# Reordering the first loads, an early load of x, and a rebuilt tail in an attention and GLU kernel

**Chip, cores, metric.** One core of one Trainium2 chip. The metric is device time in microseconds (us) of one launch. The profiled span is about 1.8 us shorter than the time of the same run (367.0 and 368.85 before).

## The reference, cut to what matters

```python
x  = A_x                                     # 1 x 2048 x 640, bf16
xn = _layernorm(x, axis=-1)
s  = _A_ref(xn, wq, wk, wv, wo, beta)        # 4 segments of 512 rows, 32 heads of 20:
                                             #   causal softmax attention in the segment
                                             #   + linear memory M, z of the segments before, gated by beta; then @ wo
g  = _silu(_B_ref(xn, w_gate, w_up, w_down)) # h = sigmoid(xn @ w_gate) * (xn @ w_up), 640 -> 1536 -> 640
return x + s * g
```

## The kernel before

Everything stands in one hand-made order per engine. A segment's attention is cut into 8 head groups of 3 units, so 24 slots per segment and 96 in all. Each slot issues the scores of one unit, the exponentials (ScalarE), planned items of the next segment, and "dense" items (gate, up and down projections) until the planned TensorE time of the slot is reached. A few functions matter here.

```python
# head: x in four pieces, then whole weights on the SP queue; Wg and Wu on the ACT queue
load_x(0, split=4)
load_w(nc.sync, Wv, A_wv); load_w(nc.sync, Wk, A_wk); load_w(nc.sync, Wq, A_wq)
# ... (cut)
for j in range(4):
    ln_transpose(0, j, xns[j], nc.scalar)
    if j < 2:
        keep_warm(3)                                   # dummy matmuls
        w, src = ((Wg, B_w_gate), (Wu, B_w_up))[j]
        load_w(nc.scalar, w, src)
    if j >= 1:
        for half in range(2):
            do_V(0, j - 1, half, nc.scalar)
# ... V of tile 3, three K groups, three Q groups (cut)
spill(0, 1, nc.sync, nc.sync)
bound(0, 1, None)
k_tok(0)            # transposing DMA
load_x(1)           # x of segment 1
do_gate(0, 0)
do_up(0, 0)
```

```python
def do_up(n, f):    # 5 matmuls into a PSUM tile; hT frees it. Three such tiles serve all dense work
    # ... (cut)
    nc.vector.scalar_tensor_tensor(out=h[:], in0=seg[n]["tg"][:], scalar=1.0, in1=up[:], op0=ALU.add, op1=ALU.mult)

# segment_plan: what slot s of segment n does for segment m = n + 1
for j in range(4):
    at(j, 0, stats, j)          # VectorE: statistics of row tile j of x
    at(4 + j, 0, norm, j)       # VectorE: normalise, then store to DRAM
at(7, 0, ln_dmaT, m)            # transposing DMA of the whole segment
```

```python
total = sum(...)                                 # planned ns of all items, dense ones too
rate = total / (NSEG * NSLOT)                    # planned TensorE ns per slot
# in every slot:
    scores(g, UNITS[ui]); pt = exps(ui, UNITS[ui])
    due += rate
    run(small); fill(due - rate / 2)             # fill: dense items until the planned time done reaches its argument
    if pend is not None: attend(*pend)           # attention of the unit before
    run(big)
    # ... (cut)
    fill(due)
# after the last slot
fill(1e12)
for j in range(4): tail_T(j)                     # transposes of the first 4 of 5 column blocks
for i in range(2): tail_mm(i)
attend(*pend)                                    # the last unit: 2 of 4 row tiles
for i in range(2, 6): tail_mm(i)
tail_end()                                       # add, last column block, last matmuls, then 8 mults and 4 adds;
                                                 # three of the adds on GpSimd, one on VectorE
```

## Time and profile before

| | before |
|---|---|
| time, first 4 runs | 369.57 us median (368.58 to 370.38) |
| profiled run | span 367.0 us |
| first scores start, 5th unit's scores start | 33.09, 49.06 |
| scores of the last (96th) unit start | 349.67 |
| from there to the end of the span | 17.33 |

In the lines of the profile PE is TensorE's matmuls, DVE VectorE, ACT ScalarE, POOL GpSimd, and SPq the DMA queue of SyncE. Sps holds the scores, pt their exponentials, Aps the attention sums, odot the finished attention, gp and up the gate and up products, tg the tanh of gp, hT the product that goes into the down projection (yp), po and oT the transposed attention.

The starts are read from the timeline of the matmuls that write the scores. They cut the span in three: a head up to the fifth unit, by which the hole at 40 us and its slow clock are over; a middle, in which TensorE (PE) is the bound; and a tail.

### The profile page before, as it was taken

How to read it: one execution, taken by the hardware profiler on the slowest of the kernel's cores; microseconds unless marked ns; L12 is line 12 of the kernel's file. 1: busy time of each engine (PE TensorE's matmuls, PEld its weight loads, DVE VectorE, ACT ScalarE, POOL GpSimd, SP SyncE). 2: the span in 40 equal slices, each digit the busy share in tenths (PEclk: the TensorE clock that was granted, in tenths of full speed). 3: DMA queues.
4: the chain of work that ended last, by engine and by line, in shares of the span. 5: the costliest groups of instructions: out<-in, count | busy, mean ns of one | idle time of the engine just before them, and what ended most of it. 6: DMA issues, size and time to landing. Idle time of an engine off the chain costs nothing.

```text
span 367.0 us, 8227 instructions
## 1 busy us (share of the span) xinstructions
PE 340.2 (93%) x3346; PEld 186.2 (51%) x3389; DVE 221.1 (60%) x499; ACT 224.4 (61%) x234; POOL 104.7 (29%) x172
## 2 busy tenths in 40 slices
PE   7999799999999898999999899999989999999992
PEld 2633344655554444555466345555436644555661
DVE  5373566554656984775746986856655573554444
ACT  2424488656776665556677666466867666666540
POOL 7600242222223242222142432222222232322224
PEclk9999899999999999999999999999999999999998
DMA  7976781311483117121393026111402023001001
GB/s 230 384 272 162 173 307 56 73 45 43 103 168 80 56 38 175 41 79 64 102 174 76 36 80 173 36 62 63 133 1 75 2 74 73 18 22 35 2 1 71
DMA packets 48309, 35.40 MB, mean 96 GB/s; under 512 B 25360, under 2 KB 46992, under 8 KB 48272
## 3 DMA queue, kind: packets, MB, share of 16 engines
q1 hardware_dynamic: 46960, 30.95, 30.4%
q10 hardware_dynamic: 1312, 3.93, 2.7%
q8 instruction: 26, 0.43, 0.5%
q14 instruction: 11, 0.09, 0.1%
HBM read 17.05 MB, written 11.80 MB: 79 GB/s over the span
## 4 chain that ended last, share of the span: by engine, by line
PE 65%; ACT 11%; DMA 7%; DVE 7%; issue 3%; SPq 3%; POOL 2%; POOLq 0%; ACTq 0%; DVEq 0%
PE yp L375 13%; PE up L361 11%; PE gp L352 9%; ACT pt L475 8%; PE Aps L491 7%; PE psq L224 6%; PE Sps L467 6%; PE sp L402 4%; PE psv L282 4%; DMA Kd<-ktd 2%; DMA Wv<-in_A_wv_dram 2%; DMA oT<-Od 1%; DMA xt<-in_A_x_dram 1%; POOL pt L477 1%; PE dm L318 1%
## 5 line engine op out<-in xcount | busy, mean ns | idle before, releaser
L475 ACT ACTIVATE pt<-Sps 128x2048 bf16<-128x2048 f32 (+1 forms) x96 | 152.9, 1592 | 50.7 <-PE Sps L467 49.9
L477 POOL TENSOR_SCALAR_AFFINE_SELECT pt<-pt 128x512 bf16<-128x512 bf16 x128 | 83.7, 664 | 247.2 <-ACT pt L475 247.0
L361 PE MATMUL up<-xnT,Wu 128*128 128x512 bf16 x225 | 58.9, 380 | 5.9 <-ACT tg L355 3.0
L352 PE MATMUL gp<-xnT,Wg 128*128 128x512 bf16 x228 | 59.4, 384 | 2.9 <-ACT tg L355 1.8
L375 PE MATMUL yp<-Wd,hT 128*128 128x320 bf16 x384 | 57.5, 299 | 0.0
L491 PEld LDWEIGHTS <-pt 128*128 128x128 bf16 x1280 | 44.3, 96 | 23.3 <-issue 4.9
L364 DVE SCALAR_TENSOR_TENSOR hT<-tg,up 128x512 bf16<-128x512 bf16 x48 | 32.6, 680 | 37.7 <-PE up L361 32.7
L491 PE MATMUL Aps<-V,pt 128*128 128x21 bf16 x1280 | 47.6, 173 | 4.1 <-DVE odot L503 1.9
L375 PEld LDWEIGHTS <-hT 128*128 128x128 bf16 x384 | 35.1, 97 | 14.9 <-issue 2.0
L355 ACT ACTIVATE tg<-gp 128x512 bf16<-128x512 f32 x48 | 28.6, 595 | 22.5 <-PE gp L352 18.9
L379 DVE SCALAR_TENSOR_TENSOR aa<-t,yp 128x320 bf16<-128x320 bf16 x32 | 15.6, 487 | 40.4 <-ACT t L378 40.3
L467 PE MATMUL Sps<-QT,KT 21*128 21x128 bf16 (+3 forms) x512 | 35.1, 303 | 1.1 <-ACT pt L475 0.8
L361 PEld LDWEIGHTS <-Wu 128*128 128x128 bf16 x240 | 21.0, 97 | 27.5 <-issue 8.5
L352 PEld LDWEIGHTS <-Wg 128*128 128x128 bf16 x240 | 20.7, 98 | 24.3 <-issue 5.9
L467 PEld LDWEIGHTS <-KT 21*128 21x128 bf16 x512 | 11.5, 91 | 33.0 <-issue 32.6
L282 PE MATMUL psv<-Wv,xnT 128*128 128x320 bf16 x160 | 26.1, 299 | 0.8 <-DMA Wv<-in_A_wv_dram 0.8
L287 ACT CAST V<-psv 128x320 bf16<-128x320 f32 x32 | 13.7, 428 | 20.4 <-PE psv L282 20.2
L224 PE MATMUL psq<-xnT,Wq 128*128 128x512 bf16 x92 | 23.7, 378 | 1.0 <-DMA Wq<-in_A_wq_dram 0.5
L224 PE MATMUL psq<-xnT,Wk 128*128 128x512 bf16 x92 | 23.6, 378 | 0.5
L378 ACT ACTIVATE t<-yp 128x320 bf16<-128x320 f32 x32 | 14.0, 437 | 16.3 <-PE yp L375 16.2
L229 DVE CAST ktd<-psq 128x512 bf16<-128x512 f32 x20 | 13.8, 688 | 14.9 <-PE psq L224 14.8
L402 PE MATMUL sp<-Wo,oT 128*128 128x320 bf16 x120 | 20.2, 298 | 1.3 <-DMA oT<-Od 1.3
(84 smaller groups left out, 316.7 us busy)
## 6 DMA issues: line engine op xcount, KB each, us to landing
KT<-Kd SPq DMA_DIRECT2D x32, 80.0 KB
QT<-Qd SPq DMA_DIRECT2D x32, 80.0 KB
out_dram<-xt SPq DMA_DIRECT2D x16, 160.0 KB
Wg<-in_B_w_gate_dram ACTq DMA_DIRECT2D x1, 1920.0 KB
Wu<-in_B_w_up_dram ACTq DMA_DIRECT2D x1, 1920.0 KB
xt<-in_A_x_dram SPq DMA_DIRECT2D x3, 640.0 KB
Wd<-in_B_w_down_dram SPq DMA_DIRECT2D x1, 1920.0 KB
Xd<-xn SPq DMA_DIRECT2D x12, 160.0 KB
```

Source lines behind the costliest of these rows:

```text
L224: nc.tensor.matmul(ps[:], lhsT=W[:, k, c * P:(c + 1) * P], rhs=xnT_of[n][:, k, :], start=(k == 0), stop=(k == DC - 1))
L282: nc.tensor.matmul(ps[:], lhsT=xnT_of[n][:, k, j * P:(j + 1) * P], rhs=Wv[:, k, half * HD:(half + 1) * HD], start=(k == 0), stop=(k == DC ...
L352: nc.tensor.matmul(gp[:], lhsT=Wg[:, k, f * P:(f + 1) * P], rhs=xnT_of[n][:, k, :], start=(k == 0), stop=(k == DC - 1))
L355: nc.scalar.activation(tg[:], gp[:], ACT.Tanh, scale=0.5)
L361: nc.tensor.matmul(up[:], lhsT=Wu[:, k, f * P:(f + 1) * P], rhs=xnT_of[n][:, k, :], start=(k == 0), stop=(k == DC - 1))
L364: nc.vector.scalar_tensor_tensor(out=h[:], in0=seg[n]["tg"][:], scalar=1.0, in1=up[:], op0=ALU.add, op1=ALU.mult)
L375: nc.tensor.matmul(yp[:], lhsT=s["hT"][f][:, j * P:(j + 1) * P], rhs=Wd[:, f, hs], start=(f == 0), stop=(f == FC - 1))
L402: nc.tensor.matmul(sp[:], lhsT=s["oT"][:, c, j * P:(j + 1) * P], rhs=Wo[:, c, hs], start=(c == 0), stop=(c == DC - 1))
L467: nc.tensor.matmul(Sps[:, r, c0:c0 + ncol], lhsT=KT[32 * r:32 * r + E1, g, kb * P:(kb + 1) * P], rhs=QT[32 * r:32 * r + E1, g, q0:L], star ...
L475: nc.scalar.activation(pt[:, :, 0:ntot], Sps[:, :, 0:ntot], ACT.Exp, scale=SCALE)
L477: nc.gpsimd.affine_select(out=pt[:, :, c0:c0 + P], in_=pt[:, :, c0:c0 + P], compare_op=ALU.is_ge, fill=0.0, base=0, pattern=[[0, 4], [1, P ...
L491: nc.tensor.matmul(Aps[:, qb, r, :], lhsT=pt[:, r, off:off + P], rhs=V[n % 2][:, kb, 4 * g + r, :], start=(ui == 0 and r == 0 and qb == 0) ...
```

## The change

The intent is to close holes of PE at both ends. The diff, cut to its core:

```diff
 # head
-    load_x(0, split=4)
-    load_w(nc.sync, Wv, A_wv)
+    for half in range(2):
+        load_x(0, ((2 * half, 2 * half + 1), (2 * half + 1, 2 * half + 2)))
+        hs = slice(half * HD, (half + 1) * HD)
+        nc.sync.dma_start(Wv[:, :, hs], A_wv[:, hs].rearrange("(c p) n -> p c n", p=P))
     ...
+    hold = cpool.tile([P, 1], BF, name="hold")
+    nc.gpsimd.tensor_copy(hold[:], xns[3][:, 0:1])    # GpSimd's constants wait for the last xn
     late_constants()
     ...
-            w, src = ((Wg, B_w_gate), (Wu, B_w_up))[j]
+        else:
+            w, src = ((Wg, B_w_gate), (Wu, B_w_up))[j - 2]
     ...                                               # V: half 0 of all row tiles first, then half 1
 # x of segment 1
     bound_dma(0, 0, [nc.sync])
+    load_x(1)
     ...
     k_tok(0)
-    load_x(1)
     ...
-            at(j, 0, stats, j)
-            at(4 + j, 0, norm, j)
-        at(7, 0, ln_dmaT, m)
+            at(j + (n == 0), 0, stats, j)
+            at(6 + j // 2 if n == 0 else 4 + j, 0, norm, j)
+        at(7 + (n == 0), 0, ln_dmaT, m)
 # two down groups kept back; total, and so rate, is computed without them
     plans = [segment_plan(n) for n in range(NSEG)]
+    held = [dense.pop() for _ in range(2)]
     total = ...
 # tail
+                if n == NSEG - 1 and slot == NSLOT - 1:
+                    tail_add(0, 2, C4, D)             # half the rows of the last group are finished early
     ...
-    fill(1e12)
-    for j in range(4):
-        tail_T(j)
     ...
+    for j in range(4):
+        tail_T(j, nc.vector if j % 2 else nc.scalar)
+    dense.extend(reversed(held))
+    fill(1e12)
+    tail_T4(0, 2); tail_mm(4, 0, DC - 1); tail_mm(5, 0, DC - 1)
+    attend(*pend)
     ...                                               # outputs in order of readiness, the last two adds on VectorE
```

So it has four parts: the head, the early x, the tail, and a side effect of the two held groups on `rate`.

More of the change, by code (lines that the diff above doesn't have):

```diff
@@ L98, with load_x @@
     xt_of, xnT_of = {}, {}
-    def load_x(n, split=1):
-        xt = lnp.tile([P, 4, D], BF, name="xt4", bufs=3)
+    def load_x(n, parts=((0, 4),)):
+        if n not in xt_of:
+            xt_of[n] = lnp.tile([P, 4, D], BF, name="xt4", bufs=3)
         src = x2[n * L:(n + 1) * L, :].rearrange("(j p) d -> p j d", p=P)
-        w = 4 // split
-        for i in range(split):
-            nc.sync.dma_start(xt[:, i * w:(i + 1) * w, :], src[:, i * w:(i + 1) * w, :])
-        xt_of[n] = xt
+        for a, b in parts:
+            nc.sync.dma_start(xt_of[n][:, a:b, :], src[:, a:b, :])
     def load_w(eng, dst, src):
@@ L416, in tail_add, with tail_T @@
         nc.vector.tensor_tensor(t, t, s["omem"][:, j0:j1, c0:c1], op=ALU.add)
-    def tail_T(j):
+    def tail_T(j, eng):
+        if j == 0:
+            tail["oT"] = fpool.tile([P, DC, L], BF, name="oT", bufs=1)
         po = ps_d.tile([P, DC - 1, P], BF, name="po", tag="d")
@@ L421, in tail_T @@
             nc.tensor.transpose(po[:, c, :], seg[NSEG - 1]["odot"][:, j, c * P:(c + 1) * P], ident[:])
-        if j == 0:
-            tail["oT"] = ptp.tile([P, 4, DC - 1, P], BF, name="pt")
-        oT = tail["oT"][:, j]
-        if j % 2:
-            nc.vector.tensor_copy(oT, po[:])
-        else:
-            nc.scalar.copy(oT, po[:])
-    def tail_acc(i):
-        return Sps[:, i, 0:HD] if i < 4 else tail["sp", i][:]
-    def tail_mm(i):
-        if i >= 4:
-            tail["sp", i] = ps_d.tile([P, HD], F32, name="sp", tag="d")
-        hs = slice((i % 2) * HD, (i % 2 + 1) * HD)
-        for c in range(DC - 1):
-            nc.tensor.matmul(tail_acc(i), lhsT=tail["oT"][:, i // 2, c, :], rhs=Wo[:, c, hs],
-                             start=(c == 0), stop=False, skip_group_check=True)
@@ L441, in tail_end @@
-    def tail_end():
-        s = seg[NSEG - 1]
-        tail_add(0, 4, C4, D)
-        po = ps_d.tile([P, 4, P], BF, name="po", tag="d")
-        for j in range(4):
-            nc.tensor.transpose(po[:, j, :], s["odot"][:, j, C4:D], ident[:])
-        oT = fpool.tile([P, DC, L], BF, name="oT", bufs=1)[:, 0, :].rearrange("p (j t) -> p j t", t=P)
-        nc.scalar.copy(oT, po[:])
-        for i in range(8):
-            if i >= 6:
-                tail_mm(i)
-            hs = slice((i % 2) * HD, (i % 2 + 1) * HD)
-            nc.tensor.matmul(tail_acc(i), lhsT=oT[:, i // 2, :], rhs=Wo[:, DC - 1, hs],
-                             start=False, stop=True, skip_group_check=True)
-        for i in range(8):
-            j, hs = i // 2, slice((i % 2) * HD, (i % 2 + 1) * HD)
-            aa, xr = s["aa"][j], xt_of[NSEG - 1][:, j, :]
-            nc.vector.tensor_tensor(aa[:, hs], aa[:, hs], tail_acc(i), op=ALU.mult)
-            if i % 2:
-                eng = nc.vector if j == 3 else nc.gpsimd
-                eng.tensor_tensor(xr, aa[:], xr, op=ALU.add)
-                out_store(NSEG - 1, j)
+        dst = tail["oT"][:, 0:DC - 1, j * P:(j + 1) * P]
@@ new lines, in tail_T, with tail_T4, tail_mm @@
+        if eng is nc.scalar:
+            nc.scalar.copy(dst, po[:])
+        else:
+            nc.vector.tensor_copy(dst, po[:])
+    def tail_T4(j0, j1):
+        po = ps_d.tile([P, 2, P], BF, name="po", tag="d")
+        for j in range(j0, j1):
+            nc.tensor.transpose(po[:, j - j0, :], seg[NSEG - 1]["odot"][:, j, C4:D], ident[:])
+        nc.scalar.copy(tail["oT"][:, DC - 1, j0 * P:j1 * P].rearrange("p (j t) -> p j t", t=P), po[:])
+    def tail_mm(i, c0, c1):
+        if i < 4:
+            tail["sp", i] = ps_d.tile([P, HD], F32, name="sp", tag="d")
+        j, hs = i // 2, slice((i % 2) * HD, (i % 2 + 1) * HD)
+        for c in range(c0, c1):
+            nc.tensor.matmul(tail_acc(i), lhsT=tail["oT"][:, c, j * P:(j + 1) * P], rhs=Wo[:, c, hs],
+                             start=(c == 0), stop=(c == DC - 1), skip_group_check=True)
@@ L464, in scores, with tail_out @@
+    def tail_acc(i):
+        return Sps[:, i - 4, 0:HD] if i >= 4 else tail["sp", i][:]
+    def tail_out(i, eng):
+        s = seg[NSEG - 1]
+        j, hs = i // 2, slice((i % 2) * HD, (i % 2 + 1) * HD)
+        aa, xr = s["aa"][j], xt_of[NSEG - 1][:, j, :]
+        nc.vector.tensor_tensor(aa[:, hs], aa[:, hs], tail_acc(i), op=ALU.mult)
+        if i % 2:
+            eng.tensor_tensor(xr, aa[:], xr, op=ALU.add)
+            out_store(NSEG - 1, j)
     def scores(g, unit):
@@ L494, in attend, with finalize @@
                                      skip_group_check=True)
-        if ui == NU - 1:
-            s = seg[n]
-            if g == 0:
-                s["odot"] = opool.tile([P, 4, D], BF, name="odot", bufs=2)
-            rd = opool.tile([P, 4, 4], F32, name="rd", bufs=3)
-            nc.vector.reciprocal(rd[:], Aps[:, :, :, DH])
-            nc.vector.tensor_tensor(rd[:], rd[:], omg[:, 4 * g:4 * g + 4].unsqueeze(1).to_broadcast([P, 4, 4]),
-                                    op=ALU.mult)
-            nc.vector.tensor_tensor(
-                s["odot"][:, :, 4 * g * DH:(4 * g + 4) * DH].rearrange("p q (r e) -> p q r e", e=DH),
-                Aps[:, :, :, 0:DH], rd[:].unsqueeze(3).to_broadcast([P, 4, 4, DH]), op=ALU.mult)
+        if n == NSEG - 1 and g == NG - 1:
+            if ui:
+                finalize(n, g, 2 * ui - 2, 2 * ui)
+        elif ui == NU - 1:
+            finalize(n, g, 0, 4)
+    def finalize(n, g, q0, q1):
+        s, Aps = seg[n], aps_of[0]
+        if g == 0:
+            s["odot"] = opool.tile([P, 4, D], BF, name="odot", bufs=2)
+        nq = q1 - q0
+        rd = opool.tile([P, 4, 4], F32, name="rd", bufs=3)
+        nc.vector.reciprocal(rd[:, 0:nq, :], Aps[:, q0:q1, :, DH])
+        nc.vector.tensor_tensor(rd[:, 0:nq, :], rd[:, 0:nq, :],
+                                omg[:, 4 * g:4 * g + 4].unsqueeze(1).to_broadcast([P, nq, 4]), op=ALU.mult)
+        nc.vector.tensor_tensor(
+            s["odot"][:, q0:q1, 4 * g * DH:(4 * g + 4) * DH].rearrange("p q (r e) -> p q r e", e=DH),
+            Aps[:, q0:q1, :, 0:DH], rd[:, 0:nq, :].unsqueeze(3).to_broadcast([P, nq, 4, DH]), op=ALU.mult)
     wps = ps_d.tile([P, L], F32, name="wps", tag="d")
@@ L531 @@
             keep_warm(3)
-            w, src = ((Wg, B_w_gate), (Wu, B_w_up))[j]
+        else:
+            w, src = ((Wg, B_w_gate), (Wu, B_w_up))[j - 2]
             load_w(nc.scalar, w, src)
         if j >= 1:
-            for half in range(2):
-                do_V(0, j - 1, half, nc.scalar)
-    for half in range(2):
-        do_V(0, 3, half, nc.scalar)
+            do_V(0, j - 1, 0, nc.scalar)
+    do_V(0, 3, 0, nc.scalar)
+    for j in range(4):
+        do_V(0, j, 1, nc.scalar)
     for c in range(3):
@@ L709 @@
             bound_dma(n + 1, 1, [nc.sync])
+    for j in range(4):
+        tail_T(j, nc.vector if j % 2 else nc.scalar)
+    dense.extend(reversed(held))
     fill(1e12)
-    for j in range(4):
-        tail_T(j)
-    for i in range(2):
-        tail_mm(i)
+    tail_T4(0, 2)
+    tail_mm(4, 0, DC - 1)
+    tail_mm(5, 0, DC - 1)
     attend(*pend)
-    for i in range(2, 6):
-        tail_mm(i)
-    tail_end()
+    tail_add(2, 4, C4, D)
+    tail_mm(0, 0, DC)
+    tail_mm(1, 0, DC)
+    tail_mm(6, 0, DC - 1)
+    tail_mm(7, 0, DC - 1)
+    tail_T4(2, 4)
+    tail_out(0, None)
+    tail_out(1, nc.gpsimd)
+    tail_mm(2, 0, DC)
+    for i in range(4, 8):
+        tail_mm(i, DC - 1, DC)
+    tail_mm(3, 0, DC)
+    tail_out(2, None)
+    tail_out(3, nc.gpsimd)
+    for i in range(4, 8):
+        tail_out(i, nc.vector)
 _INS = ['A_x', 'A_wq', 'A_wk', 'A_wv', 'A_wo', 'A_beta', 'B_x', 'B_w_gate', 'B_w_up', 'B_w_down']
```

## The prediction

> **What bounds the kernel now.** I read the page's busy shares first, then its slices, then the waits, and the timeline only where those showed a hole. Shares and slices of the kernel before:
>
> ```profile
> PE 340.2 (93%) x3346; PEld 186.2 (51%) x3389; DVE 221.1 (60%) x499; ACT 224.4 (61%) x234; POOL 104.7 (29%) x172
> ...
> PE   7999799999999898999999899999989999999992
> ...
> PEclk9999899999999999999999999999999999999998
> ```
>
> TensorE is the bound: 340.2 of 367.0 us busy, 26.8 us idle. Each digit is 9.2 us. The weak slices are the first, the fifth (36.7 to 45.9 us, PE at 7 and the only mid-kernel clock below 9) and the last. The windows view says how much is to be had where: from 46 to 345 us PE works 285.24 of 299.00 us, so nothing that the change does to the ends is lost again there unless PE stalls anew; a microsecond saved before 46 us should stay saved. The waits of the first 46 us name the holes (total us, times, longest):
>
> ```profile
> DVE st L177 <- DMA xt<-in_A_x_dram: 8.3, 2, 6.5
> ...
> PE up L361 <- DVE hT L364: 2.1, 1, 2.1
> ...
> PE psv L282 <- DMA Wv<-in_A_wv_dram: 0.8, 1, 0.8
> PE psq L224 <- DMA Wq<-in_A_wq_dram: 0.5, 1, 0.5
> ```
>
> The second is the big one, and the chain of waits in order of time explains it (start, length, what):
>
> ```profile
> 32.89 2.80 SPq L308
> 35.69 0.05 issue
> 35.74 4.66 DMA xt<-in_A_x_dram
> 40.40 0.02 issue
> 40.42 0.90 DVE st L177 x2
> ...
> 41.47 0.65 DVE hT L364
> 42.12 0.04 issue
> 42.16 1.24 PE up L361 x5
> ```
>
> The load of segment 1's x is issued at 35.74, behind the 2.80 us issue of the transposing DMA. VectorE has the statistics of that x ahead of hT in its program, stands until 40.40, and the PSUM tile that `up` needs is not freed until hT has run. PE is still from 40.06 to 42.16. Then its clock drops (windows view; third from the end is PEclk):
>
> ```profile
> 43.00:44.00 1.00, 1.00 (x19) 0.62 (x18) 1.00 (x3) 0.71 (x1) 0.22 (x1) 0.69 0.59 128
> 44.00:45.00 1.00, 0.78 (x3) 0.41 (x3) 0.96 (x4) 0.00 (x0) 0.42 (x1) 0.50 0.44 41
> 45.00:46.00 1.00, 1.00 (x7) 0.16 (x5) 1.00 (x3) 0.01 (x1) 0.00 (x0) 0.50 0.61 150
> 46.00:47.00 1.00, 1.00 (x6) 0.23 (x3) 0.31 (x2) 0.96 (x2) 0.00 (x0) 0.60 0.99 332
> ```
>
> The missing clock adds up to 0.31 + 0.50 + 0.50 + 0.40 = 1.7 us, some 1.6 us of it while PE had work. The tail (chain, last pieces): the last matmul ends at 361.54, but the add on GpSimd sets the end.
>
> ```profile
> 358.57 0.90 DVE aa L458 x2
> 359.46 0.07 issue
> 359.54 2.74 POOL xt L461 x2
> ```
>
> Three such adds (median 1391 ns each) run until 363.88; the last store is issued at 364.3 and the span ends at 367.0, 2.7 us later.
>
> [...] Wq, on the SP queue, lands only at 19.41, when by my sum of the rates some 6.1 MB had moved, though only 3.1 MB stand on its own queue up to it; the rest was Wg, issued on ACT at 6.76. [...] The normalisation of the fourth tile took 1.95 us beside GpSimd's constants, 0.39 to 0.45 otherwise.
>
> **The change part by part.**
>
> *Head, V.* x tiles 0 and 1, half of Wv, x 2 and 3, the other half, then Wk, Wq; Wg and Wu start after the third and fourth transpose copy (about 10 and 11 us instead of 6.76 and 8.11). Half of Wv then ends after 0.74 MB, reached at about 5.0 us in the windows; before, all of it landed at 9.36. PE was ready at 8.72 and waited 0.78. But the new order (V half, transpose, V half, transpose, V, V) puts one V copy (0.43 us) on ScalarE ahead of each xnT copy (0.69), so V of tile 3 must wait. Walking it: V0 8.72 to 9.40, pT2 to 9.68, xnT2 on ACT 10.05 to 10.75, V copy to 11.2, xnT3 to 11.9, V of tile 3 at 11.95 instead of 11.48. The eight V groups (0.68 each) end at about 15.35 instead of 15.64. Gain: 0.3, not 0.8. The held GpSimd constants save VectorE 1.5 us that PE does not wait for.
>
> *Head, Wq.* Before, with Wg and Wu beside it, the SP queue got about 1.2 of the 4.2 MB that moved from 8.5 to 19.4 us, under a third. In the new kernel about 0.7 MB of Wk and Wq are left when Wg starts; at the same share they take 2.4 MB of traffic, at 390 GB/s 6 us: Wq lands by about 17 us and is needed at 18.6. Gain: 0.5. PE is busy 9.95 of 10 us from 20 to 30, so both shifts pass through: 0.8 us. Total bytes are the same, so the first spill of K, issued about 0.3 us earlier, lands as before (24.8): the first scores (33.09, shifted to 32.3) come near the last row of QT, issued at 29.99 and, at the 2.27 us that the next spill took, landed at about 32.3. I take off 0.1.
>
> *Early load of x.* It is issued at about 30.6 instead of 35.74, lands at about 34, and the statistics come one slot (some 3 us) later, behind hT. The 2.1 us stall goes, and with it the slow clock: 2.1 + 1.6 = 3.7. It pushes the second spill, the transposing DMA and the second half of KT and QT about 1 us later; these are first used some 30 us on. The norms squeezed into slots 6 and 7 are still done before the transposing DMA of slot 8. I take off 0.4 for VectorE, which now has hT, statistics and phi together in slot 4 (about 3.5 us in a slot of 3.1).
>
> *Tail.* Two down groups (1.74 us each) move behind the transposes, attention of the last group is finished for half the rows early, and VectorE takes two of four adds. PE's tail work is unchanged. From the last scores (349.67) PE idles 2.1 us of 11.9 before. After, I count one stall of 0.7 us (a PSUM tile after the transposes), so PE ends about 1.4 earlier, at 360.1. But then VectorE alone has, after the last matmul, five multiplications (0.43 each) and two adds (0.53): about 3.4 us with pipeline gaps, to 363.5, where before the end of GpSimd's work was 363.88. With the same 2.7 us for the last store: gain 0.5, at most.
>
> *Pacing.* The two held groups lower the filling rate per slot by 34 ns of planned time; items shift by up to a group. No sign known; spread of about 1 us.
>
> Sum: 0.8 - 0.1 + 3.7 - 0.4 + 0.5 = 4.5 us. 369.57 - 4.5 = 365.1.
>
> **The rivals.** *A: the stall is replaced.* The early x load stands ahead of the second spill on the same queue; if x comes late all the same, or statistics behind hT delay the next hT, PE waits again and may lose its clock again. For it: the DMA share in 30 to 36 us is already uneven. Against: it is 0.08 in 30 to 31 us, and x then has 6 us. This would leave 1 us of the 3.7: about 368. *B: all holes close and the tail too.* If ScalarE copies faster than I walked, V gains 0.8, and if GpSimd's chain really was the tail's bound, its removal gains 1.5 to 2: about 363. For it: GpSimd ends 2.3 us after the last matmul. Against: the new VectorE queue ends 3.4 us after it. *C: the saving before 46 us is eaten later.* ScalarE (61%) and VectorE (60%) would have to bind in the middle. Against: the middle has PE at 95%. This would make about 368.5.
>
> **Range and chances.** My sum has about 2 us of uncertainty: the clock penalty 1, pacing 1, the tail 0.7, the head 0.5. The four runs before spread over 1.8 us. So 362.7 to 367.3. Faster by over 2% needs 362.2, 7.4 us saved, more than all holes that I count in the parts touched: 0.07. Slower needs a new stall of 12 us: 0.01.
>
> **What would show it.** Right: no wait of `up` for hT at 40 us, clock 1.00 from 40 to 47, the x load issued near 30.6, no wait for Wq, V ending near 15.3 with a wait for xnT of about 0.5; in the tail, PE ending some 3.4 us before VectorE's last add. Wrong: a half clock elsewhere (also in the head, where PE is given less to do), a PE wait for scores or for ktok, more idle time between 46 and 345 us than 13.8 us, or VectorE's tail shorter than 3 us.

## More of the kernel before

The lines of the profile on which the argument rests are in the prediction. One view that it only summed up is needed later: the waits of PE in the middle, here from 46 to 345 us of the kernel before (what waited, for what; us in total, times, longest).

```profile
PE up L361 <- ACT tg L355: 3.0, 4, 1.6
PE Aps L491 <- DVE odot L503: 1.9, 3, 0.8
PE gp L352 <- ACT tg L355: 1.8, 2, 1.3
...
PE Sps L467 <- ACT pt L475: 0.8, 2, 0.4
```

Gate and up groups wait for a PSUM tile that ScalarE's tanh has not yet read (tg): 4.8 us in 6 waits.

## The result and the profile after

| | before | after |
|---|---|---|
| time, median (range, fast runs) | 370.08 (368.58 to 371.67, 16 runs) | 362.09 (361.59 to 363.59, 10 runs; an eleventh fast one, 364.00, is not counted) |
| ratio of the fast runs | | 0.979 (0.977 to 0.981) |
| span of the profiled run | 367.0 | 360.0 |
| first scores, 5th unit's scores | 33.09, 49.06 | 31.83, 44.58 |
| last unit's scores | 349.67 | 340.10 |
| from there to the end | 17.33 | 19.90 |

A ratio is the mean time of one kernel's fast runs over that of the other's of the same rounds, so it is not quite the ratio of the medians beside it. By the ratio the change saves 7.7 us (7.0 to 8.5); a later repeat gave 6.6 (5.2 to 7.9). The prediction had 4.5, and the time lies below its range. Whether more than 2% was gained, to which it gave a chance of 0.07, stays open: 0.98 lies in the interval. Shares and slices after:

```profile
PE 337.7 (94%) x3346; PEld 186.0 (52%) x3389; DVE 221.1 (61%) x504; ACT 224.0 (62%) x235; POOL 102.7 (29%) x172
...
PE   7999999999999999999998799998989999899992
...
PEclk9999999999999999999999999999999999999997
```

The fifth slice is now 9, and so is its clock. PE is idle for 22.3 us instead of 26.8; it also has 2.5 us less busy time. Of this, 0.8 us is in the eleven dummy matmuls of the first 6 us (3.95 us of busy time there instead of 4.76; the record of the full clock begins at 4.11 us, before at 5.83), where it costs nothing. The other 1.7 us is as much as was missing of the clock before from 43.38 to 46.79 us, where it was 0.50. In the first 46 us no wait of PE for Wv, Wq or hT is left. Two other waits there are:

```profile
DVE st L178 <- DMA xt<-in_A_x_dram: 2.1, 2, 1.9
...
PE pT L201 <- DVE xn L187: 1.4, 2, 1.1
```

The timeline of VectorE shows the new order at the place of the old hole (start, length, operation; in brackets the idle time before it and what ended it):

```profile
35.05 0.69 DVE L365 SCALAR_TENSOR_TENSOR hT<-tg,up 128x512 bf16<-128x512 bf16 x1 [2.36 <-ACT tg L356]
...
35.89 0.89 DVE L178 BATCH_NORM_STATS2 st<-xt 128x6 f32<-128x320 bf16 x2 [0.16 <-DMA xt<-in_A_x_dram]
```

hT runs first, and the statistics follow at 35.89 after a wait of only 0.16 us, where before they started at 40.42 and hT at 41.47. The load was issued at 31.05 (predicted: near 30.6). The windows view gives the full clock where it was 0.69 and 0.50:

```profile
43.00:44.00 1.00, 1.00 (x13) 0.58 (x12) 0.53 (x1) 1.00 (x1) 0.00 (x0) 1.00 0.71 134
44.00:45.00 1.00, 1.00 (x13) 0.31 (x11) 0.95 (x3) 0.57 (x2) 0.64 (x1) 1.00 0.70 123
```

The end of the chain that ended last, after:

```profile
352.83 0.69 PE sp L442 x5
...
353.54 1.29 DVE aa L452 x3
...
354.86 0.99 DVE xt L454
355.85 0.81 DVE aa L452 x2
...
356.68 0.49 DVE xt L454
```

VectorE now ends the kernel, 3.65 us after PE's last matmul (353.52 to 357.17; predicted about 3.4). The first of its two adds takes 0.99 us and the second 0.49. The first runs while GpSimd adds too (GpSimd's takes 1.39 us from 354.11). It is the same in the trace of e12 (0.99 beside an add of GpSimd, 0.49 after it). In the head, too, VectorE was slower beside GpSimd: the normalisation of the fourth tile, 1.95 us beside GpSimd's constants before, takes 0.45 after, where they are held.

**Where the 7.0 us of the two spans came from.** The fifth unit starts 4.5 us earlier: 1.26 of that is there at the first scores (head, or chance: e1 below has the old head, happens to wait for neither Wv nor Wq, and starts at 31.81 as well), 3.2 come after it (x). The middle, from the fifth unit to the last, takes 295.52 instead of 300.61; 3.3 of these 5.09 us are the two held down groups (2 x 1.64, the median from the start of a group's 12 matmuls to the start of what follows), which merely moved; 1.8 us are saved. The tail takes 19.90 with those 3.3 us in it, so 16.6 like for like, 0.7 less than 17.33. Head and x were predicted at 4.0 together (0.8 − 0.1 + 3.7 − 0.4). What the prediction did not have is mainly the 1.8 us in the middle:

The waits of PE in the middle, after (46 to 340 us):

```profile
PE up L362 <- ACT tg L356: 2.3, 4, 1.0
PE Aps L484 <- DVE odot L503: 2.2, 2, 1.4
...
PE Sps L460 <- ACT pt L468: 1.6, 4, 0.4
...
PE gp L353 <- ACT tg L356: 0.5, 1, 0.5
```

The waits of gate and up for tanh fell from 4.8 to 2.8 us; those of attention and scores rose by 0.3 and 0.8. From the fifth scores to the last PE is idle for 12.26 us in all, before for 13.76. The work is the same, but for the two groups, and it stands differently in the slots.

### The profile page after: what moved, and what is told of

It is laid out like the page before. It is cut to its first block, busy times and chain, and to the rows that moved or that the text cites.

```text
span 360.0 us, 8234 instructions
## 1 busy us (share of the span) xinstructions
PE 337.7 (94%) x3346; PEld 186.0 (52%) x3389; DVE 221.1 (61%) x504; ACT 224.0 (62%) x235; POOL 102.7 (29%) x172
## 3 DMA queue, kind: packets, MB, share of 16 engines
q1 hardware_dynamic: 47616, 30.95, 30.6%
## 4 chain that ended last, share of the span: by engine, by line
PE 78%; ACT 9%; DVE 5%; issue 2%; DMA 2%; POOL 2%; ACTq 0%; SPq 0%; POOLq 0%
PE up L362 13%; PE yp L376 13%; PE gp L353 13%; PE psq L225 10%; PE Aps L484 8%; PE Sps L460 7%; ACT pt L468 6%; PE sp L403 5%; PE psv L283 4%; DMA oT<-Od 2%; PE cps L269 2%; PE dm L319 1%; PE am L338 1%; DVE st L178 1%; ACT tg L356 1%
## 5 line engine op out<-in xcount | busy, mean ns | idle before, releaser
L470 POOL TENSOR_SCALAR_AFFINE_SELECT pt<-pt 128x512 bf16<-128x512 bf16 x128 | 82.8, 657 | 237.5 <-ACT pt L468 237.5
```

The source lines that it names most:

```text
L470: nc.gpsimd.affine_select(out=pt[:, :, c0:c0 + P], in_=pt[:, :, c0:c0 + P], compare_op=ALU.is_ge, fill=0.0, base=0, pattern=[[0, 4], [1, P ...
```

## The experiments

The theory that follows from the stretches: the early x gives some 3 us and more, through the stall and its slow clock; the new tail and the lower `rate` give the rest, each about 1; the head comes on top only when x is early. The rivals: the tail alone gives the rest and `rate` nothing; the parts simply add up, the head too; or the clock, whose loss varies from run to run (granted clock in the fast runs of before: 0.986 to 0.996), is worth more than one trace of each kernel shows. The runs came in four jobs, e1 to e4, e5 to e8, e9 to e12, e13 and e14, each on one chip. The expectations, as they were written before each run, say what was thought by then.

Every timed run of an experiment is compared with the kernel before on the same chip. "us" worked out from a ratio is (1 − ratio) times the median of before there (369.3 to 369.5).

### Each part alone, and the change without x

**e1**, only the early x, on the kernel before:

```diff
     bound_dma(0, 0, [nc.sync])
+    load_x(1)
     k_tok(0)
-    load_x(1)
-            at(j, 0, stats, j)
-            at(4 + j, 0, norm, j)
-        at(7, 0, ln_dmaT, m)
+            at(j + (n == 0), 0, stats, j)
+            at(6 + j // 2 if n == 0 else 4 + j, 0, norm, j)
+        at(7 + (n == 0), 0, ln_dmaT, m)
```

> The kernel before with only the early load of segment 1's x and the statistics and norms of segment 0 one or two slots later. By the account of the two traces (slot 2 of the scores: TensorE 2.57 us less idle, 1.73 us less missing clock, of which 0.30 us of idle belongs to the head) this part alone is worth 3.2 us in the profiled pair: ratio about 0.991. Rival: the stall returns in another place once the head is as before; then ratio 0.997 to 1.0. Second rival: the clock penalty of the kernel before is larger in other runs than in the profiled one, then 4 to 5 us, ratio 0.987 to 0.989, and the runs of this kernel spread less than those of before (3.1 us).

Measured: 364.46 us (363.93 to 368.74, 6 runs), ratio 0.9888 (0.9848 to 0.9927), so 4.1 us. No wait of PE for hT, no clock below 1.00 up to 50 us; the fifth unit starts at 44.38, as in the whole change.

**e2**, the whole change with the x load, statistics and norms put back (the reverse of that diff):

> The changed kernel with the load of x, the statistics and the norms put back where they were. If the parts add up, it loses what e1 gains: about 3.2 to 5 us over the changed kernel, so a ratio to before of 0.988 to 0.992, a wait of up for hT of about 2 us near 40 us and half clock after it. If the early head alone already hides the late x, it loses under 1 us (ratio 0.981).

Measured: 367.82 us (20 runs), ratio 0.9956 (0.9942 to 0.9971): 1.6 us are left of 6.6 to 7.7. The wait of PE up to 50 us:

```profile
PE up L362 <- DVE hT L365: 4.3, 1, 4.3
```

So with the new head a late x stalls PE for twice as long as before, and 3.41 us of clock are missing instead of 1.71 (0.9 of them while PE stands still anyway). Taking the x part out of the whole costs 5 to 6 us; putting it in alone brings 4.1 (2.7 to 5.6). That the parts are not independent is shown by the next run.

**e3**, only the head (Wv in halves, V order, Wg and Wu late, `hold`) on the kernel before:

> The kernel before with only the new loads, order and holds of the first 15 us (Wv in halves, Wg and Wu later, constants held). In the traces the first scores come 1.26 us earlier. If it stays: ratio 0.9965. But x of segment 1 is still issued behind the transposing DMA, whose place depends on spills that did not move earlier, so the stall at 40 us grows by what the head gained: then ratio 0.999 to 1.0 and a stall of about 3.3 us. I hold the second for likelier: the two parts are worth more together than each alone.

Measured: 370.2 us (22 runs), ratio 1.0024 (1.0009 to 1.0039): 0.9 us **slower**. First scores at 31.78, as in the whole change, so its 1.3 us are there. Then PE comes to the hole earlier, and x does not: it is issued at 35.65 (before 35.74). The wait, and one line of the windows view, in which the clock is third from the end:

```profile
PE up L362 <- DVE hT L365: 3.5, 1, 3.5
```

```profile
47.00:48.00 1.00, 1.00 (x6) 0.24 (x6) 0.00 (x0) 0.76 (x2) 0.00 (x0) 0.50 1.05 392
```

The stall ends at about the same time (42.3, before 42.2) and the half clock lasts from 41.2 to 48.0: 3.41 us missing, 1.7 more than before, 0.6 of them inside the stall. Over all fast runs of the job the missing clock is 4.2 us, against 3.6 in the kernel before. The head's gain is eaten by the wait, and more slow clock makes it a loss.

**e4**, only the tail with its two held groups, and so with the lower rate:

> The kernel before with only the new tail, with the two down groups held back (so also the slower filling rate). By the account of the traces the end after the last scores is worth 0.9 us and the middle 1.5 us, if the filling rate is what changed the middle: ratio 0.9935. If the middle gained because of the earlier start, only the 0.9 us remain: 0.9975.

Measured: 366.58 us (19 runs), ratio 0.9924 (0.9903 to 0.9945), so 2.8 us (2.0 to 3.6), where the prediction had 0.5 for the tail and nothing for the rate. Its profiled run started badly (PE waited 2.7 us for Wq and 1.7 for Wv), but its middle took 295.70 us from the fifth to the last scores, like the whole change's 295.52. The wait for Wq was followed by half clock (22.17 to 25.58). The stall before hT was 2.2 us in it, and the clock stayed full. So a stall of 2.1 us cost 1.7 us of clock in before, and one of 2.2 us nothing here.

The traces show a difference between the two. In before the clock changes at 5.833, 43.380, 46.793 and 364.233 us; the distances, 37.547, 3.413 and 317.440 us, are 11, 1 and 93 times 3.413. In after it changes at 4.112 and 355.685, which is 103 times that apart, and the half clock of e4 lasted 3.41. So I cut each trace into windows of 3.413 us that end where its clock changes; they lie elsewhere in each of the three (the first ends at 2.42, 0.70 and 1.69 us). Here are the two windows at the stall, first in before, then in e4 (PE's busy time is the first number after the comma):

```profile
39.97:43.38 3.41, 1.31 (x15) 0.72 (x12) 2.89 (x8) 1.18 (x2) 0.56 (x1) 1.00 0.71 147
43.38:46.79 3.41, 3.19 (x26) 1.08 (x24) 2.89 (x8) 1.09 (x3) 0.64 (x1) 0.50 0.63 147
```

```profile
42.65:46.06 3.41, 1.97 (x27) 0.99 (x25) 0.97 (x3) 1.14 (x1) 1.23 (x2) 1.00 0.82 240
46.06:49.47 3.41, 2.67 (x30) 1.29 (x29) 3.34 (x10) 1.51 (x2) 0.64 (x1) 1.00 0.61 111
```

In before one window holds the whole stall of 2.10 us, and the next one gets half clock. In e4 the boundary at 46.06 cuts the stall into 1.44 and 0.74 us, and the clock stays full. In the rest of before and after, half clock followed the two windows in which PE's work ends (2.69 us idle from 360.82 in before, 2.18 from 352.27 in after), and none of the others, which have up to 1.62 us (from 357.41 in before) and 1.40 (from 202.09 in after). After the stalls of 3.5 and 4.3 us (e3, e2) it lasted 6.8 us. One case in e11 does not fit: half clock from about 203.6 to 207.1 after a wait of only 1.42 us; it stays open. For before and e4, then, the difference is how much of the stall fell into one window. No part of either kernel was placed with regard to the windows, so I count that as chance.

Together: e1 4.1 + e4 2.8 = 6.9 us, and the head between −0.9 (alone) and about +1. e2 is e4 with the new head, and 1.2 us slower by the ratios: the loss of e3 once more. The whole is 6.6 to 7.7. The surprise is e4, and it has two parts of its own.

### The rate

**e5**, only the lower rate, on the kernel before: the same items in the same queue, tail as it was, but 34 ns less planned work per slot.

```diff
-    rate = total / (NSEG * NSLOT)
+    rate = (total - 2 * DN_NS) / (NSEG * NSLOT)
```

> The kernel before with nothing changed but the filling rate: the planned total is lowered by the two down groups (as the changed kernel does by holding them back), so the dense matmuls are spread later over the slots and the last of them run after the last scores. e4 (tail and rate together) gained 2.8 us, of which the two traces give the tail proper 0.4 to 0.9 us. If the rate is the rest, this gains 1 to 2 us: ratio 0.995 to 0.997, and TensorE's idle time between slots 15 and 94 falls by 1 us or more below that of e1 and e3 (11.2 to 11.5 us). If the rate does nothing and the tail was worth the whole: ratio 1.0.

Measured: 368.74 us (22 runs), ratio 0.9974 (0.9955 to 0.9992), so 1.0 us (0.3 to 1.7). The middle took 295.74 us. The waits of PE in it (51 to 345 us):

```profile
PE up L361 <- ACT tg L355: 2.3, 4, 1.0
...
PE gp L352 <- ACT tg L355: 0.5, 1, 0.5
```

These are the figures of the kernel after. In this respect the traces fall into two classes. Six kernels with the old rate (before, e1, e3, e6, e7, e13) all have 3.0 and 1.8 for these two waits, 1.9 for Aps behind odot and 0.8 for Sps behind pt, to the tenth. Nine with the lower rate (after, e2, e4, e5, e8 to e12) all have 2.3, 0.5, 2.2 and 1.6. The sum is 7.5 against 6.6 us. From the fifth scores to the last, before, e1, e3 and e13 take 300.45 to 300.78 us, and after, e2, e4, e5, e8, e9, e10 and e12 take 295.52 to 295.84 and the two groups' 3.3 (done after the last scores in all of these), so 298.8 to 299.1: 1.3 to 2.0 us of gain, of which these waits explain 0.9; the rest I have not located. (e7 has the old pattern and took 299.41, for its wait for the transposed oT was 0.2 us instead of 1.1 to 1.5. e11 lost 1.7 us of clock near 205 us, and e6 comes next.)

**e6**, the whole change with the old rate:

```diff
-    rate = total / (NSEG * NSLOT)
+    rate = (total + 2 * DN_NS) / (NSEG * NSLOT)
```

> The changed kernel with the two held groups counted in the rate again, so that the slots are filled as in the kernel before and only the tail's order is new. If the rate is worth 1 to 2 us, the ratio to before is 0.982 to 0.985 against 0.979 for the changed kernel; if it is worth nothing, 0.979.

Measured: 367.59 us (22 runs), ratio 0.9948 (0.9929 to 0.9967), some 5 us worse than the change. Up to 344 us it has the old pattern of waits, but it is no pure undoing of the rate: dense work is now used up one slot early, and the last scores had to wait for the exponentials:

```profile
344.98 0.29 PE L460 MATMUL Sps<-QT,KT 21*128 21x256 bf16 x4 [1.53 <-ACT pt L468]
```

Two shorter waits for GpSimd follow, and then about 1.7 us of clock are missing from 346 to 350. So e6 says that the held groups and the lower rate belong together; it does not size the rate.

**e14**, the rate of the kernel before lowered further, to see whether there is a trend:

```diff
-    rate = total / (NSEG * NSLOT)
+    rate = (total - 5 * DN_NS) / (NSEG * NSLOT)
```

> The kernel before with the planned total lowered by five down groups instead of two, so that five groups (8.7 us of TensorE) instead of two run after the last scores. If a slower filling rate is better in itself, slots 3 to 94 shrink by more than the three further groups moved out (5.2 us) from the 295.7 us of the rate lowered by two. If the 1.6 us that the middle gained are the luck of which group falls beside which wait, it differs by a microsecond either way, and the waits of up and gp for tg, of attention for odot and of the scores for pt change their lengths without a trend. Time against before: between 0.994 and 1.002.

Measured: 374.08 us (5 fast runs; a sixth, 381.32 at a granted clock of 0.929, was slow), ratio 1.0112 (1.0082 to 1.0142): 4.1 us slower. What costs the 4.1 us stays open. A lower rate is thus not better in itself; the step of the change happened to fall well.

### The tail by itself

**e13**, the new tail on the kernel before, but with nothing held back and so with the old rate:

```diff
-    held = [dense.pop() for _ in range(2)]
+    held = []
+    fill(1e12)
     for j in range(4):
         tail_T(j, nc.vector if j % 2 else nc.scalar)
-    dense.extend(reversed(held))
-    fill(1e12)
```

> The kernel before with the new order of the tail (last group finished in two halves, two adds on GpSimd and two on VectorE), but no down groups held back and the old filling rate. e4 (all of the tail and the rate) was worth 2.8 us, e5 (the rate alone) 1.0. If the tail's order is a part of its own: 0.9 to 1.8 us, ratio 0.995 to 0.9975, and slots 3 to 94 take 300.5 us as in all kernels with the old rate. If the order needs the held groups to fill its waits (the transposes' PSUM tiles, the last copy of attention), TensorE stands still longer after the last scores and under 0.5 us is gained: ratio 0.999.

Measured: 368.28 us (11 fast runs; a twelfth, 373.53, was slow), ratio 0.996 (0.9936 to 0.9983), so 1.5 us (0.6 to 2.4). In its trace the middle takes 300.45 us (as before) and the tail 16.49 instead of 17.33, so 0.84. The tail part and the rate part, 1.5 and 1.0, make the 2.8 of e4 within their intervals.

**e11**, the changed kernel with its last steps in another order: the matmuls of one more output ahead of the four closing ones, all multiplications first, and the two VectorE adds last.

```diff
+    tail_mm(3, 0, DC)
     for i in range(4, 8):
         tail_mm(i, DC - 1, DC)
-    tail_mm(3, 0, DC)
     ...
-    for i in range(4, 8):
-        tail_out(i, nc.vector)
+    for i in range(4, 8):
+        tail_out(i, None)      # multiplication only
+    for j in range(2, 4):
+        tail_sum(j)            # add and store
```

**e12** is the change itself once more, on the same chip.

> The changed kernel with a shorter end: the last matmul group of the second row block comes before the four closing matmuls of the other accumulators, and VectorE makes all multiplications first and its two adds last. In the changed kernel's trace VectorE works 3.67 us after the last matmul, and its first add takes 0.99 us beside GpSimd's, the second 0.49 alone. This should take 0.5 us from the order of matmuls and 0.5 us from the add: 1.0 us faster than the changed kernel, ratio 0.976. If the end hangs on the stores rather than on VectorE: under 0.3 us.

> The changed kernel itself, on the same chip as e9 to e11, to compare them with it directly: ratio 0.979 (0.977 to 0.981), and a spread of its runs of about 2 us.

Measured: e11 361.15 us (360.71 to 362.16), ratio 0.9783 (0.9747 to 0.9818); e12 362.16 (361.66 to 363.93), ratio 0.9822 (0.9786 to 0.9859). The chain of e11 at its end:

```profile
354.35 0.56 PE Sps L442 x4
...
354.93 1.68 DVE aa L452 x4
...
356.61 0.40 DVE xt L459
```

And the last line of its timeline of VectorE:

```profile
356.53 0.89 DVE L459 TENSOR_TENSOR xt<-aa,xt 128x640 bf16<-128x640 bf16 x2
```

PE's last matmul ends at 354.91 and VectorE at 357.42, 2.5 us later and not 3.65; the two adds take 0.89 together, none of them 0.99. From the last scores to the end it is 18.81 us, in e12 19.87, so 1.06 less. The medians say 1.0, the intervals of the two ratios overlap. This order of the tail is probably about 1 us better; it is the best of all kernels run.

### The clock by itself

**e7**, the kernel before with x late as it was, but with 18 dummy matmuls into columns of the score tile that are free then, at the place of the hole:

```diff
                 scores(g, UNITS[ui])
+                if n == 0 and slot == 2:
+                    for _ in range(18):
+                        nc.tensor.matmul(Sps[:, 0, 256:512], lhsT=ident[:], rhs=Wk[:, 0, 0:256], start=True, stop=True)
```

> The kernel before with 18 extra matmuls (128 contracted rows, 256 columns, about 0.11 us each, into unused columns of the score banks) right where TensorE stands still for x near 40 us. The stall stays, only the array is kept busy. If the slow clock after the stall costs time of its own, this is faster than before by what the clock lost on average in the runs (mean missing clock 3.6 us per run of before against 2.4 of the changed kernel, so about 1.3 to 2 us): ratio 0.995 to 0.9965, and no clock under 1.00 between 42 and 48 us. If the lost clock is hidden by other waits: ratio 1.0.

The 0.11 us is an estimate: half of the 0.22 at which matmuls of 512 columns follow each other in the trace of before (five in 1.09 us).

Measured: 366.94 us (9 runs), ratio 0.9934 (0.9912 to 0.9957), so 2.4 us (1.6 to 3.3), with x as late as ever. Its wait and one of its windows:

```profile
PE up L361 <- DVE hT L364: 1.5, 1, 1.5
```

```profile
44.00:45.00 1.00, 1.00 (x17) 0.56 (x14) 1.00 (x3) 0.24 (x1) 0.63 (x1) 1.00 0.22 46
```

The clock is full where it was 0.50. The missing clock over a whole run (1 less the granted clock, times the span) averages 3.6 us in the 110 fast runs of the kernel before in the first three jobs, and 1.8 us in this kernel; it is 1.9 in e1 and 2.4 in the whole change. These averages contain what is missing after the last matmul, which costs nothing (1.4 us in the trace of before, 2.4 in that of e7), so 3.6 does not say that the hole cost more than the 1.7 us of the trace. In those runs of before, time goes with missing clock (correlation 0.68, slope 0.79 us per us). The hole is still there, so most of the gain is the worth of the clock: 1.8 us of it were won back. The 2.4 by ratio agree within their interval, but need not be clock alone, for in this one trace the wait for oT in the middle was also about 1 us shorter.

### The parts of the head, once x is early

**e8**, the change with Wg and Wu issued early as before; **e10**, the change with Wv whole and the old order of V; **e9**, the change without any of the head (early x and tail only).

```diff
 # e8
-        else:
-            w, src = ((Wg, B_w_gate), (Wu, B_w_up))[j - 2]
+            w, src = ((Wg, B_w_gate), (Wu, B_w_up))[j]        # in the branch j < 2
 # e10
-    for half in range(2): ...                                 # x and Wv in turns
+    load_x(0, ((0, 1), (1, 2), (2, 3), (3, 4)))
+    load_w(nc.sync, Wv, A_wv)                                 # and V by row tile, both halves
```

> The changed kernel with Wg and Wu issued where they were before (after the first two transpose copies). Then Wv's second half and Wq have to share the DMA engines with 3.9 MB again. If that sharing is what the head's gain comes from: the wait for Wq comes back (0.5 us in the profile of before, 2.7 us in that of e4), with a wait for Wv's second half: 0.5 to 1.5 us slower than the changed kernel, ratio 0.980 to 0.983. If it is only the earlier V start, 0.979 stays.

> The changed kernel with the old head (x in four loads, then Wv whole; Wg and Wu early; nothing held), so the early x and the tail together. e1 and e4 add up to a ratio of 0.981. Across the profiles the first scores come at 31.7 to 37.7 us with the old head (five profiles, mean 33.8) and at 31.8 to 32.4 with the new one (five, mean 32.0). If that holds on average the head is worth 1 to 1.8 us once x is early: ratio 0.982 to 0.984, with a wider spread than the changed kernel. If the two slow starts among the profiles were chance, under 0.5 us: 0.980.

> The changed kernel with Wv loaded whole after all of x, and V computed in the old order; Wg, Wu and the constants stay late. e8 showed that early Wg and Wu cost nothing while Wv is in halves. If it is enough that either of the two is done, this equals the changed kernel within 0.3 us: 0.979. If the halves are what the head gains by: 0.5 to 1 us slower, 0.981 to 0.982.

| | median (us) | ratio to before | first scores in the trace |
|---|---|---|---|
| e8 | 362.02 | 0.9803 (0.9771 to 0.9834) | 32.35 |
| e9 | 363.05 | 0.9834 (0.9796 to 0.9872) | 32.13 |
| e10 | 362.4 | 0.9823 (0.9789 to 0.9856) | 33.36 |
| e12 (the change) | 362.16 | 0.9822 (0.9786 to 0.9859) | 32.08 |

None of these differs from the change beyond its interval. The late Wg and Wu bring nothing that could be seen. The whole head is worth 0.4 us by the ratios and 0.9 by the medians, not resolved from zero. What the traces do show is spread: with the old head the first scores start anywhere from 31.7 (e7) to 37.7 us (e4), depending on when Wv and Wq arrive (waits of up to 2.7 us for Wq and 1.7 for Wv, both in e4); with the whole new one, in six traces, from 31.8 to 32.1.

## Why the prediction was wrong

Its mechanism for x and the place of the largest gain were right. Its total of 4.5 us was too small by 2 to 3.

| step | predicted | measured |
|---|---|---|
| early x | 3.7 − 0.4 = 3.3 | 4.1 by ratio (e1), 3.2 between the two traces |
| head | 0.8 − 0.1 = 0.7 | 1.26 between the two traces, perhaps chance; −0.9 alone (e3); 0.4 to 0.9 once x is early (e9), not resolved |
| tail | 0.5 | 1.5 by ratio (0.6 to 2.4), 0.84 in the trace (e13) |
| pacing | 0 | 1.0 by ratio (0.3 to 1.7, e5), 1.8 between the two traces |

**The step that failed most** is "Pacing. ... No sign known; spread of about 1 us". I looked in the middle for new stalls only, and not for old ones that could go. There were 4.8 us of waits for tanh, 2 of which went with the new placing. With "gain 0.5, at most" for the tail it makes 0.5 us in the prediction against 2.8 in e4. No sign could have been read from the profile of before, and e14 shows that a step two and a half times as large has the opposite one; so the honest figure was zero with a wider spread than 1 us, in a range that should have reached lower. The split of the 2.8 between tail and rate stays loose.

**The tail.** The working held in its form: PE stalls 0.42 us after the transposes (I had 0.7), and VectorE ends 3.65 us after PE (3.4). It moves 0.7 to 0.9 us in traces; "at most" was wrong by a little. I compared the end of VectorE's work (363.5) with the end of GpSimd's (363.88), though the kernel ends with the last store, which I had at 364.3: in before it stands behind GpSimd's store on the SP queue (issued at 363.90 and 364.33), and after it goes out at 357.19, 0.02 us after VectorE's last add. The two groups take 1.64 us each on PE, not 1.74.

**The clock** was sized from one trace: 1.6 us. As a size that held: the missing clock falls by 1.7 us on the mean in e1, by 1.8 in e7 and by 1.2 in the whole change. That it goes when the stall goes was read from the same place, where the half clock began 1.2 us after the stall. But the size was luck, since stalls of 2.1 and 2.2 us lost 1.7 us (before) and nothing (e4); the four times of before, 1.8 us apart, hinted at that, and a term seen in one run should have had a spread of its own size. The half clock lasted from 43.38 to 46.79.

**The head** was added as if independent. Before x was early, its 0.8 us could not "pass through": the hole at 40 us ends when x lands, so PE only waits longer (3.5 us instead of 2.1, to 42.3 instead of 42.2), and e3 shows it to be worth less than nothing. After x is early, what it saves can pass through, but e9 does not resolve it from zero, and the 1.26 us between the traces of before and after may be chance (e1 has no wait for Wv or Wq with the old head). I had the two in one sum in an order in which that was harmless; a reader who took the head alone from it would have been wrong. In the reading of the queues "the rest was Wg" is not quite so: 2.93 MB had moved on the ACT queue by 19.41 us, and Wg is 1.97 of them, so some of Wu was among it.

**The rivals.** A (stall replaced) did not come: e1 and the change show no wait for hT. B (all holes and the tail too, 363) was nearest in number; its stated reasons were V and GpSimd's chain. The tail's gain was of that kind and half that size, the head gained more than I walked (first K group at 14.92 instead of 15.48, so 0.56 and not 0.3; first Q group at 18.16 instead of 19.41, so 1.25 and not 0.8), and the rest was pacing, which no rival had. C (saving eaten in the middle) was the reverse of what happened.

## What to carry to other kernels

Here a stall that ended when a load landed swallowed the 1.3 us saved before it, and returned them as a longer stall with more slow clock (e3: 3.5 us instead of 2.1, 1.7 us more clock missing, 0.9 us slower): remove the stall first and judge the earlier savings afterwards. In a hand-placed schedule a change of the pacing is a part of the change like any other; run it alone, and expect a change of either sign (1.0 us faster in e5, 4.1 slower in e14), since several short waits can come or go together (7.5 or 6.6 us here). Size a clock loss from the granted clock of many runs, not from one trace, since a stall of 2.1 us cost 1.7 us in one trace and one of 2.2 nothing in another. Where a hole can't be closed, dummy matmuls into unused PSUM columns may buy back the clock that it costs; in the trace of e7 they filled only a part of it (1.5 us of idle time were left), and that was enough there (clock 1.00 from 40 to 49 us, 2.4 us faster by ratio).
